# Attention and experts on one core: spreading weight scales by DMA and loading raw weights in halves

## The chip, the cores and the metric

The kernel runs on one core of a Trainium2 chip. The metric is the device time of one execution in microseconds (us). The engines are named as the profile names them: PE (matmuls), DVE (VectorE), ACT (ScalarE), POOL (GpSimd) and SP (SyncE, which here only issues DMAs).

## What is computed

A block-sparse attention over 4 batches, 8 heads, 768 tokens and 64 channels a head, and then a layer of 8 experts, of which every token passes through all, weighted by a balanced matrix P.

```python
scores = scale * np.matmul(q, k.transpose(0, 1, 3, 2))
scores = np.where(mask, scores, -1000000000.0)
attn = softmax(scores)                       # over keys
x = (attn @ v) as (3072, 512)
P = exp(logits - max); 8 times: P /= row sums, P /= column sums, P *= N / E
for e in range(8):
    h = np.maximum(x @ w1[e], 0.0)           # w1[e] is 512 x 1024
    ye = h @ w2[e]                           # w2[e] is 1024 x 512
    out += P[:, e:e + 1] * ye
```

(The reference's softmax and the balancing are shortened here; in all else it is the above in NumPy, in float32.)

## The kernel before

The attention comes first, written out as a list of steps by time slots. It gives x, which is split into seven combinations of its quadrants (a scheme with seven products in place of eight) and stored in DRAM as pairs of float16 planes (`xd`): a high part and the rest. The experts follow. For each of the 8 experts and 4 batches (32 rounds of 384 + 384 tokens) stage 1 multiplies x by w1 and stage 2 multiplies the result h by w2, each with seven products of float16 planes, and each product as three matmuls (high by high, high by low, low by high). From the third expert on, four of the seven products of stage 1 are cut once more into seven smaller ones (`inner_product`, the matmuls of L1608; the others are L1579). The matmuls of stage 2 are L1931. DVE and ACT read the products out of PSUM, form sums, and DVE or POOL make the low planes of h (L1797, L1799, L1814).

The weights arrive in float32. For each expert and each of w1 and w2 (functions `fetch_w1` and `fetch_w2`):

- `raw_load` issues one DMA of 2 MB into the one raw buffer (L421), when all readers of the weights that stood there before are done.
- `scale_jobs` finds the largest magnitude. ACT sums magnitudes in 8 parts, one after the other (L351). DVE takes each partition's maximum of the 8 (`whole`, L438). PE transposes that column (`spread`, L357), with a PSUM bank of stage 1 (`hold("s1")`) as its target, so that each partition sees all 128. DVE takes the maximum (L444) and makes a power of two and its inverse (L445 to L451, `power`).
- POOL forms the differences and sums of the quadrants in place (L1321). `split_jobs` makes each of seven planes: ACT the high half (L1333, with the scale), DVE the low half (L1338).
- `weight_job` multiplies P's column by the two inverse scales (DVE, L1453 to L1457).

None of this stands at a fixed place. A small planner (`Plan`) gets each piece of work as a job with its engine, an assumed duration, the jobs it depends on and a deadline, goes through time, and lets each engine take the ready job with the nearest deadline. PE has two streams, stage 1 and stage 2, each in its own fixed order, and takes the head that is due first. Some jobs may go to DVE or POOL, whichever is free first. A job with `rush` goes ahead of all. The outcome is one list, and every engine runs its instructions in the order of that list. So an edit of the jobs changes the order on all engines. DMAs of SP are issued in order too: one that waits holds those behind it.

Of the kernel before, what the change touches and what calls it, by code (L numbers as in the profile page):

```python
# [9 lines left out]
F32 = mybir.dt.float32  # L10
# [10 lines left out]
P = 128  # L21
# [16 lines left out]
PREP0, PREP1, PREPD = 100, 190, 50  # L38
TWO1 = ()
LOFT = 31  # L40
STEP = 2.03
# [256 lines left out]
def tile_sparse_attention_moe(  # L298
# [117 lines left out]

    def load_w(which, e):
        src, n, w = (w1, KD, FF) if which == 1 else (w2, KF, DM)
        t = raw.tile([P, KD * FF], F32, tag="r", name=f"r{which}_{e}")
        t = t.rearrange("p (c f) -> p c f", f=w)  # L420
        nc.sync.dma_start(out=t, in_=src[e].rearrange("(c p) f -> p c f", p=P))  # L421
        wr[which] = t

    def scale_steps(which, e, vector=nc.vector, scalar=nc.scalar):
# [9 lines left out]
        def part(k):  # L434
            magnitude(scalar, m[:, k : k + 1], flat[:, k * w : (k + 1) * w])
# [16 lines left out]

        return [lambda k=k: part(k) for k in range(n)], whole, spread, power

# [137 lines left out]
    with ExitStack() as actx:  # L592
# [477 lines left out]
        def start_w():  # L1070
            load_w(1, 0)
            parts, whole, spread, power = scale_steps(1, 0)
# [63 lines left out]
    def spare(n):  # L1136
# [13 lines left out]
        [dram.tile([P, CH, DM], F32, name=f"accd_{b}_{j}") for j in range(2)] for b in range(B)  # L1150
    ]
    xsd = [dram.tile([P, NP, 2, 4, TH // 2], F16, name=f"xsd_{b}") for b in range(B)]

# [134 lines left out]
    last_s3 = [()]  # L1288
    raw_free = [()]
    pwe = {}  # L1290

    def raw_load(which, e):
        return plan.dma(lambda: load_w(which, e), 2048, raw_free[0])

    def scale_jobs(which, e, loaded):
        cell = {}

        def make():
            cell["steps"] = scale_steps(which, e)

        parts = []
# [22 lines left out]
    def tts(out, x, y, n, deps, dur, op=ALU.subtract):  # L1324
        return [
            tt(lambda k=k: out()[:, k], lambda k=k: x()[:, k], lambda k=k: y()[:, k], deps, dur, op)
            for k in range(n)
        ]

    def split_jobs(which, e, dst, src, deps):  # L1330
        s = lambda: wr["s", which]
        hi = job(
# [12 lines left out]
    def fetch_w1(e):  # L1345
# [6 lines left out]

        loaded = job({"-": 0.0}, views, (loaded,) + tuple(last_s3[0]))
# [12 lines left out]
        def inner(p, src, deps):  # L1366
# [8 lines left out]
            part = lambda l: sums[p][:, l].rearrange("p (k i) f -> p k (i f)", k=KH)  # L1375
            s = lambda: wr["s", 1]
            hi = job(
# [25 lines left out]
        put(4, q10, d_s1)  # L1403
        last_s3[0] = tuple(out[5])
        raw_free[0] = tuple(x for p in out for x in out[p])
        split_done[1, e] = out

    def fetch_w2(e, loaded=None, done=None):
# [7 lines left out]

        if e == 0 or loaded is None:
            if loaded is None:
                loaded = raw_load(2, e)
            start = job({"-": 0.0}, views, (loaded,) + tuple(last_s3[0]))  # L1420
            parts, _ = scale_jobs(2, e, start)
        else:
            start = job({"-": 0.0}, views, (loaded,))
            parts = [start]
            scaled[2, e] = start
        g = lambda k: (lambda: r[k])
        m00, m10, m01, m11, t1 = (g(k) for k in ((0, 0), (1, 0), (0, 1), (1, 1), "t1"))
        base = tuple(parts)
        out = {}
# [4 lines left out]

        d_t1 = tts(t1, m01, m00, h2, base, 0.73)
# [4 lines left out]
        d6 = tts(m01, m01, m11, h2, tuple(d_t1), 0.73)  # L1440
        six = put(6, m01, d6)
# [4 lines left out]
        last_s3[0] = tuple(four)  # L1446
        raw_free[0] = tuple(x for p in out for x in out[p])
        split_done[2, e] = out
# [438 lines left out]
    def stage2(i, t0, length):  # L1887
# [6 lines left out]
        loaded = {}  # L1894
        fresh = e == 0 or 2 <= e < NE - 1
        if not fresh:
# [230 lines left out]
```

## Time and profile before

| what | us |
|---|---|
| median of 3 runs (lowest to highest) | 2171.04 (2168.24 to 2175.3) |
| the profiled execution's own time | 2168.09 |
| its span | 2166.0 |
| PE busy | 2115.0 |
| DVE busy | 1728.0 |
| ACT busy | 1442.7 |
| POOL busy | 1168.6 |

The span runs from the first to the last instruction; the time of the execution holds some 2 us around it. An engine's busy time is the union of its instructions; a matmul's record lasts longer than the time after which the next one starts. In a row of waits stand the waiting engine, line and tile, whom it waited for, the total, the number of waits and the longest. In a row of the timeline stand start, duration, engine, line and operation, and in brackets the idle time before it and who ended it. In a row of windows stand the stretch, its length, the busy time of PE, PE's weight loads, DVE, ACT and POOL (with the number of instructions), the granted clock, the share of the DMA engines and GB/s.

### The profile page before, as it was taken

The page shows a single profiled execution, that of the slowest core. Times are in us where ns is not written, and L with a number is a line of the kernel's source. Part 1 is how long each engine was busy: PE and PEld are TensorE (multiplying, and loading weights), DVE is VectorE, ACT ScalarE, POOL GpSimd, SP SyncE. Part 2 cuts the span into 40 slices and gives each one's busy share as a digit, 9 for nine tenths or more (in the row PEclk, how much of TensorE's full clock was granted, in tenths as well). Part 3 has the DMA queues.
Part 4 walks back from the last instruction along what each step waited for, and adds up shares of the span by engine and source line. Part 5 has one row for each costly group of instructions (what it writes and reads, how often), then busy time and mean ns, then how long its engine had stood idle before and what let it go on. Part 6 is the DMA issues. An engine that isn't in the chain of part 4 may idle for free.

```text
span 2166.0 us, 51169 instructions
## 1 busy us (share of the span) xinstructions
PE 2115.0 (98%) x20620; PEld 1708.6 (79%) x20620; DVE 1728.0 (80%) x3093; ACT 1442.7 (67%) x2773; POOL 1168.6 (54%) x1343
## 2 busy tenths in 40 slices
PE   6999999899999999999999999999999999999999
PEld 3777676667777778788888888888888888888887
DVE  8878888688788878876877788778877887788776
ACT  4788888786567666666676667656665666566442
POOL 5556768465245547554655475545454545466433
PEclk9999999999999999999999999999999999999999
DMA  7667966432454643454445444545454535455421
GB/s 172 142 133 168 210 131 140 146 113 95 139 185 148 221 157 122 162 145 114 113 132 159 115 120 125 163 110 147 98 164 111 143 88 178 110 153 157 140 96 66
DMA packets 223650, 299.57 MB, mean 138 GB/s; under 512 B 134812, under 2 KB 153268, under 8 KB 223412
## 3 DMA queue, kind: packets, MB, share of 16 engines
q1 hardware_dynamic: 217088, 264.81, 41.4%
q0 software_dynamic: 5760, 31.46, 8.2%
q8 instruction: 161, 2.64, 0.5%
q14 instruction: 77, 0.63, 0.1%
q10 hardware_dynamic: 564, 0.03, 0.0%
HBM read 197.16 MB, written 67.63 MB: 122 GB/s over the span
## 4 chain that ended last, share of the span: by engine, by line
PE 89%; DVE 7%; issue 1%; DMA 1%; ACT 1%; POOL 0%; DVEq 0%; ACTq 0%; POOLq 0%; SPq 0%
PE y L1931 38%; PE p L1579 22%; PE p L1608 14%; PE u L963 4%; PE t L901 2%; PE t L898 2%; PE m L865 2%; PE m L868 2%; DVE top L874 1%; DVE acc L1970 1%; DMA qt<-qs 1%; DVE w2p L1338 1%; DVE h L1799 0%; PE u L994 0%; DVE pl L916 0%
## 5 line engine op out<-in xcount | busy, mean ns | idle before, releaser
L1931 PE MATMUL y<-w2p,h 128*128 128x256 f16 x8064 | 969.8, 273 | 3.9 <-DVE w2p L1338 2.4
L1931 PEld LDWEIGHTS <-h 128*128 128x128 f16 x8064 | 786.5, 98 | 122.8 <-issue 3.9
L1797 POOL TENSOR_TENSOR h<-pair,h 128x384 f16<-128x384 f32 x388 | 389.6, 1023 | 507.6 <-ACT h L1808 449.2
L1808 ACT ACTIVATE h<-pair 128x384 f16<-128x384 f32 x640 | 312.4, 515 | 74.6 <-DVE pair L1552 25.3
L1579 PE MATMUL p<-arena 128*128 128x384 f16 x1728 | 323.1, 326 | 1.4 <-DVE pair L1552 1.4
L1552 DVE SCALAR_TENSOR_TENSOR pair<-p,pair 128x384 f32<-128x384 f32 x384 | 213.2, 555 | 127.6 <-PE p L1579 124.5
L1970 DVE SCALAR_TENSOR_TENSOR acc<-y,spare,acc 128x256 f32<-128x256 f32 x408 | 201.7, 496 | 125.3 <-PE y L1931 123.7
L1793 ACT ACTIVATE pair<-pair 128x384 f32<-128x384 f32 x384 | 195.1, 517 | 142.1 <-DVE pair L1552 115.4
L1579 PEld LDWEIGHTS <-arena 128*128 128x128 f16 x1728 | 166.9, 98 | 83.7 <-issue 1.8
L874 DVE TENSOR_REDUCE top<-m 128x1 f32<-128x768 f32 x192 | 181.9, 951 | 49.3 <-PE m L868 48.5
L906 ACT ACTIVATE pe<-t,qk 128x768 int32<-128x768 f32 x192 | 172.3, 899 | 70.6 <-PE t L901 63.2
L1608 PEld LDWEIGHTS <-loft 128*128 128x128 f16 x2304 | 198.9, 98 | 23.8 <-issue 8.6
L1579 PE MATMUL p<-attic 128*128 128x384 f16 x1152 | 214.3, 326 | 0.0
L1958 ACT ACTIVATE acc<-y,spare 128x256 f32<-128x256 f32 (+1 forms) x180 | 97.9, 544 | 134.7 <-PE y L1931 134.3
L1608 PE MATMUL p<-loft 128*128 128x192 f16 x1728 | 176.6, 246 | 6.7 <-DVE pair L1661 3.7
L1579 PEld LDWEIGHTS <-attic 128*128 128x128 f16 x1344 | 130.6, 98 | 66.6
L1839 POOL TENSOR_TENSOR pair<-pair,pair 128x384 f32<-128x384 f32 x111 | 123.3, 1123 | 90.5 <-DVE pair L1839 72.3
L1797 POOL TENSOR_TENSOR h<-u,h 128x384 f16<-128x384 f32 x122 | 120.8, 1001 | 73.1 <-ACT h L1808 67.1
L1561 ACT ACTIVATE u<-p 128x384 f32<-128x384 f32 x216 | 105.3, 488 | 68.8 <-PE p L1608 63.0
L865 PE MATMUL m<-kt,qt 128*128 128x512 f16 (+1 forms) x384 | 127.8, 333 | 10.0 <-DMA kt<-ks 7.0
L1561 ACT ACTIVATE pair<-p 128x384 f32<-128x384 f32 x168 | 82.0, 489 | 82.7 <-PE p L1579 39.1
L1321 POOL TENSOR_TENSOR r<-r 128x256 f32<-128x256 f32 (+1 forms) x150 | 127.8, 861 | 16.2 <-DVE attic L1338 10.2
(237 smaller groups left out, 3942.6 us busy)
## 6 DMA issues: line engine op xcount, KB each, us to landing
arena<-xd SPq DMA_DIRECT2D x128, 384.0 KB, 3.3
attic<-xd SPq DMA_DIRECT2D x96, 384.0 KB, 3.3
loft<-xsd SPq DMA_DIRECT2D x96, 384.0 KB, 4.6
r<-in_moe_w_dram SPq DMA_DIRECT2D x16, 2048.0 KB, 9.5
accd<-acc POOLq DMA_DIRECT2D x40, 768.0 KB, 8.2
accd<-acc SPq DMA_DIRECT2D x16, 768.0 KB, 3.9
acc<-accd SPq DMA_DIRECT2D x16, 768.0 KB, 4.7
xd<-loft SPq DMA_DIRECT2D x28, 384.0 KB, 3.0
```

What stands on the lines that cost most here:

```text
L865: nc.tensor.matmul(sc[:, lo:hi], lhsT=qt[:, 0, c], rhs=ka[:, lo:hi], start=True, stop=False)
L874: nc.vector.tensor_reduce(out=tops[n][:, c : c + 1], in_=sc[:, :S], axis=AX.X, op=ALU.max)
L906: nc.scalar.activation(pe, sc[:, :S], AF.Exp, bias=EXP_SHIFT, scale=qk[n // 2][3])
L1552: lambda: nc.vector.scalar_tensor_tensor(out=out_(), in0=bank_(), scalar=HDOWN, in1=add(), op0=ALU.mult, op1=ALU.add),
L1561: lambda: nc.scalar.activation(out_(), bank_(), AF.Relu if relu else AF.Copy, scale=HDOWN),
L1579: nc.tensor.matmul(bk.tile[:, :TH], lhsT=w1p[p][:, l, kc, fs], rhs=xp[p][:, r, kc], start=(fresh and kc == 0 and m == 0), stop=(kc == KH - ...
L1608: nc.tensor.matmul(bk.tile[:, c * HT : (c + 1) * HT], lhsT=lhs(l, c), rhs=rhs(rr), start=(fresh and c == 0 and m == 0), stop=(m == 2), ski ...
L1793: return job({"ACT": 0.52}, lambda: nc.scalar.activation(view(), view(), AF.Relu), dep)
L1797: nc.gpsimd.tensor_tensor(out=out_, in0=x, in1=y, op=ALU.subtract)
L1808: lambda: nc.scalar.activation(h.tile[:, 0], src(), AF.Relu if relu else AF.Copy),
L1931: nc.tensor.matmul(py, lhsT=hh[i, p, kc].tile[:, l, tsl], rhs=w2p[p][:, r, kc], start=(old is None and kc == 0 and m == 0), stop=(kc == h2 ...
L1970: lambda dst=dst, src=src, t=t: nc.vector.scalar_tensor_tensor(out=dst(), in0=src(), scalar=pwe[e][:, t : t + 1] if e else 1.0, in1=dst(), ...
```

## The change

1. *Scales.* For the 15 weight matrices that the planner handles (all but the first w1), PE's transpose is gone. The column of 128 maxima is written to a DRAM tile (`peak_d`, 4 bytes a partition), and a second DMA reads it back broadcast to all partitions (`peaks`, 128 x 128). Both are issued by SP. DVE's `power` then reads `peaks` in place of a PSUM bank, and has lost `rush`.
2. *Loads.* There is one fixed raw tile, loaded by two DMAs of 1 MB, the second half of the rows first. Each half has its own list of readers that must be done (`raw_free[0]`, `raw_free[1]`). The first w1 is still loaded whole, as is the first w2.
3. *Dependencies.* The 8 magnitude parts no longer wait for each other; each waits for its half, and the parts of the second half are listed first. The differences that only read the raw weights (w1's s3, w2's t1) start when the halves have landed, without waiting for the magnitudes; those that overwrite wait for them. The scale is looked up for its own expert (`wr["s", which, e]`), as the next one may be made before the last use.
4. *ADDS* names the expert number 2 that stood in `stage2`; its value is the same.

The core of the diff:

```diff
-    def load_w(which, e):
+    def load_w(which, e, half=None):
         src, n, w = (w1, KD, FF) if which == 1 else (w2, KF, DM)
-        t = raw.tile([P, KD * FF], F32, tag="r", name=f"r{which}_{e}")
-        t = t.rearrange("p (c f) -> p c f", f=w)
-        nc.sync.dma_start(out=t, in_=src[e].rearrange("(c p) f -> p c f", p=P))
+        if "raw" not in wr:
+            wr["raw"] = raw.tile([P, KD * FF], F32, name="raw_w")
+        t = wr["raw"].rearrange("p (c f) -> p c f", f=w)
+        cs = slice(0, n) if half is None else slice(half * n // 2, (half + 1) * n // 2)
+        nc.sync.dma_start(out=t[:, cs], in_=src[e].rearrange("(c p) f -> p c f", p=P)[:, cs])
...
     def raw_load(which, e):
-        return plan.dma(lambda: load_w(which, e), 2048, raw_free[0])
+        return [
+            plan.dma(lambda j=j: load_w(which, e, j), 1024, raw_free[j]) for j in (1, 0)
+        ][::-1]
...
-        parts = []
-        last = job({"-": 0.0}, make, (loaded,))
-        for k in range(8):
-            last = job({"ACT": 0.81}, lambda k=k: cell["steps"][0][k](), (last,))
-            parts.append(last)
+        made = job({"-": 0.0}, make, (loaded[1],))
+        parts = [
+            job({"ACT": 0.81}, lambda k=k: cell["steps"][0][k](), (made, loaded[k // 4]))
+            for k in (4, 5, 6, 7, 0, 1, 2, 3)
+        ]
         whole = job({"DVE": 0.16}, lambda: cell["steps"][1](), parts)
-        bk = hold("s1", ordered=False)
-        def spread():
-            spread_bank[0] = lambda nm: bk.tile
-            cell["steps"][2]()
-        pe = job({"PE": 0.3}, spread, (whole,), take=(bk,), lag=2.0)
-        power = job({"DVE": 1.2}, lambda: cell["steps"][3](), (pe,), drop=(bk,), rush=True)
+        out_ = plan.dma(
+            lambda: nc.sync.dma_start(out=peak_d[which - 1], in_=cell["steps"][4]), 1, (whole,)
+        )
+        def back():
+            nc.sync.dma_start(
+                out=peaks[which - 1],
+                in_=peak_d[which - 1].rearrange("p one -> (p one)").unsqueeze(0).to_broadcast([P, P]),
+            )
+            wr["all", which] = peaks[which - 1]
+        in_ = plan.dma(back, 64, (out_,))
+        power = job({"DVE": 1.2}, lambda: cell["steps"][3](), (in_,))
...
-        base = tuple(parts)
-        d_s3 = tts(s3, q00, q10, KH, base, 1.27)
-        d_s1 = tts(q10, q10, q11, KH, tuple(d_s3), 1.27, ALU.add)
+        base = (seen,)
+        d_s3 = tts(s3, q00, q10, KH, (seen, loaded[0]), 1.27)
+        d_s1 = tts(q10, q10, q11, KH, tuple(d_s3) + tuple(parts), 1.27, ALU.add)
...
-        raw_free[0] = tuple(x for p in out for x in out[p])
+        raw_free[0] = tuple(x for p in (0, 4, 5) for x in out[p])
+        raw_free[1] = tuple(x for p in (1, 2, 3) for x in out[p]) + tuple(d_s1)
```

`fetch_w2` is changed in the same way. Since some DVE work is now planned at other times, 40 of the jobs that may run on either engine stand on POOL instead of DVE: 19 low planes of h, 18 pieces of the prepared x and 3 sums.

The order at three places, all at the w2 of the third expert. On PE before (`y` is stage 2's bank, `p` a bank of stage 1), between the last matmuls of a stage 2 group and those of an inner product:

```order
L1931 LDWEIGHTS h_8024
L1931 MATMUL y_8018<-w2p_8006,h_8024 128x256
L357 MATMUL p_8011<-ident,ma_w_2_13391 128x128
L1608 LDWEIGHTS attic
L1608 MATMUL p_8011<-attic 128x192
L1608 LDWEIGHTS attic
L1608 MATMUL p_8011<-attic 128x192
```

and on PE now, where the first product with the new w2 begins (`w2p_8004`; the second name of a matmul is what it streams):

```order
L1943 LDWEIGHTS h_8035
L1943 MATMUL y_8017<-w2p_8005,h_8035 128x256
L1943 LDWEIGHTS h_8040
L1943 MATMUL y_8015<-w2p_8004,h_8040 128x256
L1943 LDWEIGHTS h_8040
L1943 MATMUL y_8015<-w2p_8004,h_8040 128x256
```

No transpose stands between matmuls any more, and no bank `p` is taken for it.

On DVE before, from the last two accumulations (`acc`) through the scale (`ma_w`, `sw`, `iw`) and the expert's weights (`pc`, `pcb`, `spare`) to a sum that PE waits for (`pair` from bank `p`):

```order
L1970 SCALAR_TENSOR_TENSOR acc_8058<-y_8018,spare_10890,acc_8058 128x256
L444 TENSOR_REDUCE ma_w_2_13391<-p_8011 128x1
L445 TENSOR_SCALAR ma_w_2_13391<-ma_w_2_13391 128x1
L447 TENSOR_SCALAR ma_w_2_13391<-ma_w_2_13391 128x1
L448 RECIPROCAL sw_2_13392<-ma_w_2_13391 128x1
L450 TENSOR_SCALAR sw_2_13392<-sw_2_13392 128x1
L451 TENSOR_SCALAR iw_2_13393<-ma_w_2_13391 128x1
L1453 TENSOR_SCALAR pc_13607<-iw_2_11804,iw_2_13393 128x1
L1455 TENSOR_SCALAR pcb_13609<-inv_v,pc_13607 128x4
L1457 TENSOR_TENSOR spare_13611<-pw,pcb_13609 128x24
L1661 SCALAR_TENSOR_TENSOR pair_8045<-p_8011,u_8055 128x2x192
L1814 SCALAR_TENSOR_TENSOR h_8020<-pair_8050,h_8020 128x384
```

and on DVE now:

```order
L447 TENSOR_REDUCE ma_w_2_13202<-peaks_8069 128x1
L448 TENSOR_SCALAR ma_w_2_13202<-ma_w_2_13202 128x1
L450 TENSOR_SCALAR ma_w_2_13202<-ma_w_2_13202 128x1
L451 RECIPROCAL sw_2_13203<-ma_w_2_13202 128x1
L453 TENSOR_SCALAR sw_2_13203<-sw_2_13203 128x1
L454 TENSOR_SCALAR iw_2_13204<-ma_w_2_13202 128x1
L1982 SCALAR_TENSOR_TENSOR acc_8057<-y_8015,spare_11032,acc_8057 128x256
L1465 TENSOR_SCALAR pc_13582<-iw_2_11646,iw_2_13204 128x1
L1467 TENSOR_SCALAR pcb_13584<-inv_v,pc_13582 128x4
L1469 TENSOR_TENSOR spare_13586<-pw,pcb_13584 128x24
L1859 SCALAR_TENSOR_TENSOR p_8010<-p_8010,pair_8043 128x384
L1351 SCALAR_TENSOR_TENSOR w2p_8004<-raw_w,sw_2_13203,w2p_8004 128x1024
```

The same nine instructions stand there, but one accumulation is between them, another sum follows them, and the low part of the first w2 plane comes before the last two accumulations of the old w2, which are the next two rows. Ahead of the nine, 14 DVE instructions now lie between the local maximum (L438, now L441) and the read of the peaks; before there were nine.

On SP before, around the load of that w2 (`r` is the raw buffer, `xd` and `xsd` are x planes in DRAM, `accd` the sums in DRAM):

```order
L421 DMA r_2_13171<-in_moe_w_dram 128x8x512
L472 DMA attic<-xd_77 128x1536
L1486 DMA loft<-xsd_8068 128x1536
L472 DMA arena<-xd_77 128x1536
L1998 DMA accd_1_8066<-acc_8057 128x1536
L472 DMA arena<-xd_77 128x1536
```

and on SP now:

```order
L424 DMA raw_w<-in_moe_w_dram 128x4x512
L475 DMA attic<-xd_77 128x1536
L1498 DMA loft<-xsd_8071 128x1536
L475 DMA arena<-xd_77 128x1536
L1316 DMA peak_d_8067<-ma_w_2_13202 128x1
L475 DMA arena<-xd_77 128x1536
L1320 DMA peaks_8069<-peak_d_8067 128x128
L475 DMA attic<-xd_77 128x1536
L2010 DMA accd_1_8065<-acc_8056 128x1536
```

The load is the second of two halves (the first stands five rows above), and the two small DMAs stand among the loads of x planes, here with one of those between them.

More of the change, by code (lines that the diff above doesn't have):

```diff
@@ L39 @@
 TWO1 = ()
+ADDS = 2
 LOFT = 31
@@ L451, in power @@
             vector.tensor_scalar(inv, a, 1.0 / top, None, ALU.mult)
-        return [lambda k=k: part(k) for k in range(n)], whole, spread, power
+        return [lambda k=k: part(k) for k in range(n)], whole, spread, power, a
     KB = 1024
@@ L1071, in start_w @@
             load_w(1, 0)
-            parts, whole, spread, power = scale_steps(1, 0)
+            parts, whole, spread, power, _ = scale_steps(1, 0)
             WORK.update((part, (0.0, 0.8, 0.0)) for part in parts)
@@ L1151, in tile_sparse_attention_moe @@
     ]
+    peak_d = [dram.tile([P, 1], F32, name=f"peak_d_{n}") for n in range(2)]
+    peaks = [sk.tile([P, P], F32, name=f"peaks_{n}") for n in range(2)]
     xsd = [dram.tile([P, NP, 2, 4, TH // 2], F16, name=f"xsd_{b}") for b in range(B)]
@@ L1288, in tile_sparse_attention_moe @@
     last_s3 = [()]
-    raw_free = [()]
+    raw_free = {0: (), 1: ()}
     pwe = {}
     def raw_load(which, e):
-        return plan.dma(lambda: load_w(which, e), 2048, raw_free[0])
+        return [
+            plan.dma(lambda j=j: load_w(which, e, j), 1024, raw_free[j]) for j in (1, 0)
+        ][::-1]
     def scale_jobs(which, e, loaded):
@@ L1299, in make @@
             cell["steps"] = scale_steps(which, e)
[L1301 to L1314 removed]
+            wr["s", which, e] = wr["s", which]
+        made = job({"-": 0.0}, make, (loaded[1],))
[3 more added lines that the diff above has]
+        ]
+        whole = job({"DVE": 0.16}, lambda: cell["steps"][1](), parts)
+        out_ = plan.dma(
[9 more added lines that the diff above has]
+        power = job({"DVE": 1.2}, lambda: cell["steps"][3](), (in_,))
         scaled[which, e] = power
@@ L1330, in split_jobs @@
     def split_jobs(which, e, dst, src, deps):
-        s = lambda: wr["s", which]
+        s = lambda: wr["s", which, e]
         hi = job(
@@ L1351, in views @@
             a["s3"] = wr["s3"]
-        loaded = job({"-": 0.0}, views, (loaded,) + tuple(last_s3[0]))
+        seen = job({"-": 0.0}, views, (loaded[1],) + tuple(last_s3[0]))
         parts, power = scale_jobs(1, e, loaded)
@@ L1375, in inner @@
             part = lambda l: sums[p][:, l].rearrange("p (k i) f -> p k (i f)", k=KH)
-            s = lambda: wr["s", 1]
+            s = lambda: wr["s", 1, e]
             hi = job(
@@ L1403, in fetch_w1 @@
         put(4, q10, d_s1)
-        last_s3[0] = tuple(out[5])
-        raw_free[0] = tuple(x for p in out for x in out[p])
+        last_s3[0] = tuple(out[5]) + tuple(d_s4)
+        raw_free[0] = tuple(x for p in (0, 4, 5) for x in out[p])
+        raw_free[1] = tuple(x for p in (1, 2, 3) for x in out[p]) + tuple(d_s1)
         split_done[1, e] = out
@@ L1415, in views @@
             r["t1"] = raw.tile([P, h2, DH], F32, tag="s3", name=f"t1_{e}")
[L1417 to L1421, printed above, removed]
-        else:
-            start = job({"-": 0.0}, views, (loaded,))
-            parts = [start]
-            scaled[2, e] = start
+        if loaded is None:
+            loaded = raw_load(2, e)
+        else:
+            loaded = [loaded, loaded]
+        seen = job({"-": 0.0}, views, (loaded[1],) + tuple(last_s3[0]))
+        parts, _ = scale_jobs(2, e, loaded)
         g = lambda k: (lambda: r[k])
         m00, m10, m01, m11, t1 = (g(k) for k in ((0, 0), (1, 0), (0, 1), (1, 1), "t1"))
-        base = tuple(parts)
+        base = (seen,)
         out = {}
@@ L1433, in put @@
             return out[p]
-        d_t1 = tts(t1, m01, m00, h2, base, 0.73)
+        d_t1 = tts(t1, m01, m00, h2, (seen, loaded[0]), 0.73)
         one = put(1, m10, base)
@@ L1439, in fetch_w2 @@
         five = put(5, m00, d5)
-        d6 = tts(m01, m01, m11, h2, tuple(d_t1), 0.73)
+        d6 = tts(m01, m01, m11, h2, tuple(d_t1) + tuple(parts), 0.73)
         six = put(6, m01, d6)
@@ L1446, in fetch_w2 @@
         last_s3[0] = tuple(four)
-        raw_free[0] = tuple(x for p in out for x in out[p])
+        raw_free[0] = tuple(x for p in (0, 5, 6) for x in out[p]) + tuple(d3)
+        raw_free[1] = tuple(x for p in (1, 2, 3) for x in out[p]) + tuple(d5) + tuple(d6)
         split_done[2, e] = out
@@ L1894, in stage2 @@
         loaded = {}
-        fresh = e == 0 or 2 <= e < NE - 1
+        fresh = e == 0 or ADDS <= e < NE - 1
         if not fresh:
```

## The prediction

> **What bounds the kernel now.** I read the page first, for who is busy and who ends last.
>
> ```profile
> span 2166.0 us, 51169 instructions
> PE 2115.0 (98%) x20620; PEld 1708.6 (79%) x20620; DVE 1728.0 (80%) x3093; ACT 1442.7 (67%) x2773; POOL 1168.6 (54%) x1343
> PE 89%; DVE 7%; issue 1%; DMA 1%; ACT 1%; POOL 0%; DVEq 0%; ACTq 0%; POOLq 0%; SPq 0%
> ```
>
> PE is busy for 98% of the span and is 89% of the chain that ended last. So the kernel is a stream of matmuls, and an edit gains only if it takes instructions out of PE's queue or shortens a stall of PE. The change touches the expert stage alone, so next I asked for the busy time of that stretch, and then for what PE waited for.
>
> ```profile
> 437.00:2164.00 1727.00, 1706.78 (x15139) 1418.30 (x15137) 1373.25 (x2513) 1105.85 (x2296) 900.82 (x944) 1.00 0.46 135
> PE p L1608 <- DVE u L1645: 5.7, 5, 2.7
> PE p L1608 <- DVE pair L1661: 4.2, 5, 2.6
> PE y L1931 <- DVE w2p L1338: 2.4, 2, 1.9
> PE p L1608 <- DVE ma_w L444: 0.7, 1, 0.7
> ```
>
> In 1727.0 us PE is busy 1706.8 (the first number behind the length), so all its idle time there is 20.2 us. That is the ceiling for stalls, plus a little for slowed clock. The named waits are all for DVE: none is for a weight DMA. DVE is busy for 1373 of the 1727 us, so it has room on average, and PE stalls where DVE has a knot. I therefore looked for knots that the scaling of weights makes.
>
> **Term 1, the transposes.** Fifteen PE transposes of the weights' peaks leave PE's queue.
>
> ```profile
> L357 PE MATMUL p<-ident,ma_w 128*128 128x128 f32 x15 | 4.1, 273 | 0.0
> 441.44 0.27 PE L357 MATMUL p<-ident,ma_w 128*128 128x128 f32 x1
> 441.55 0.98 PE L1579 MATMUL p<-arena,attic 128*128 128x384 f16 x5
> ```
>
> A record lasts 273 ns, but the next matmul starts 0.11 us later, so a transpose costs PE 0.11 us. Fourteen make 1.5 us; the fifteenth is in term 2. The bounds are 1.5 and the 4.1 of the group's busy time. I take 1.5, because the starts show what the queue pays.
>
> **Term 2, the knot at 898 us**, where the scale of the third expert's w2 is made. PE first, then DVE, then the clock.
>
> ```profile
> 898.62 0.27 PE L357 MATMUL p<-ident,ma_w 128*128 128x128 f32 x1
> 899.55 0.66 PE L1608 MATMUL p<-attic 128*128 128x192 f16 x6 [0.67 <-DVE ma_w L444]
> 902.84 0.96 PE L1608 MATMUL p<-loft 128*128 128x192 f16 x6 [2.63 <-DVE pair L1661]
> 904.50 0.37 PE L1931 MATMUL y<-w2p,h 128*128 128x256 f16 x1 [0.48 <-DVE w2p L1338]
> 900.36 0.21 DVE L1453 TENSOR_SCALAR pc<-iw,iw 128x1 f32<-128x1 f32 x1
> 900.61 0.83 DVE L1455 TENSOR_SCALAR pcb<-inv_v,pc 128x4 f32<-128x4 f32 x1
> 901.47 0.84 DVE L1457 TENSOR_TENSOR spare<-pw,pcb 128x24 f32<-128x24 f32 x1
> 902.24 0.55 DVE L1661 SCALAR_TENSOR_TENSOR pair<-p,u 128x384 f32<-128x384 f32 x1
> 900.00:910.00 10.00, 6.89 (x60) 5.77 (x58) 9.03 (x18) 5.91 (x9) 5.63 (x8) 0.83 0.20 80
> ```
>
> The transpose holds a PSUM bank until DVE's L444 has read it, so the next product waits 0.67 us. Then DVE works through the scale and the three instructions of the expert's weights (to 902.3) before L1661, for which PE waits 2.63 us; then 0.48 more for the w2 plane. That is 3.78 us of idle. Behind it the granted clock of these 10 us is 0.83, which loses 1.7 us more. So the knot costs about 5.5 us. In the new order no PSUM bank is held, and the same nine DVE instructions stand further ahead of the plane's first product, with one accumulation among them. They are not gone: nine instructions and a 1.3 us plane still stand in a row ahead of that product. I leave 1.2 us of stall there and take a gain of 4.3; the bounds are 0 (the knot only moves) and 5.5.
>
> The Trainium skill, "TensorE: Matmul & The Clock Gate", section on the HAM clock gate, says that the clock halves after at least one idle window of about 3.4 us. By that rule gaps of 2.6 us would cost no clock and this term would be an estimated 2.6 instead of 4.3; the trace differs, since 0.83 follows a gap of 2.63 us, and I go by the trace.
>
> **Term 3, two smaller stalls tied to weights.**
>
> ```profile
> 719.93 0.70 PE L1931 MATMUL y<-w2p,h 128*128 128x256 f16 x5 [1.90 <-DVE w2p L1338]
> 717.94 1.94 DVE L1338 SCALAR_TENSOR_TENSOR w2p<-t,sw,w2p 128x1024 f16<-128x1024 f32 x1
> 1118.54 0.66 PE L1608 MATMUL p<-attic 128*128 128x192 f16 x6 [0.28 <-DVE pair L1661]
> 1120.06 0.66 PE L1608 MATMUL p<-loft 128*128 128x192 f16 x6 [0.86 <-DVE pair L1661]
> ```
>
> The first is a w2 plane of the second expert whose low part DVE began only as PE asked for it. Halves that are freed and loaded separately let the magnitudes start earlier, so I expect the planes earlier: bounds 0 and 1.9, taken 1.0. The second (1.14 us) comes behind the same block of DVE instructions, one expert on: bounds 0 and 1.1, taken 0.6.
>
> **What I cost at nothing, and its cover.** The magnitudes on ACT and the differences on POOL stay in number; they may start after a half has landed instead of after the whole or after all magnitudes. About 40 instructions go from DVE to POOL (low halves of h, and of the prepared x). A low half costs POOL more than DVE:
>
> ```profile
> L1797 POOL TENSOR_TENSOR h<-pair,h 128x384 f16<-128x384 f32 x388 | 389.6, 1023 | 507.6 <-ACT h L1808 449.2
> L1799 DVE SCALAR_TENSOR_TENSOR h<-pair,h 128x384 f16<-128x384 f32 x124 | 93.3, 764 | 3.8 <-ACT h L1808 3.8
> ```
>
> POOL takes 1.02 us against 0.76. PE's work on other planes hides it, and POOL idles half the time. Were the cover gone, 40 times 0.26 us is 10 us. The DVE time that is freed (40 times at most 0.76, 30 us) is worth nothing by itself, as DVE has 20% to spare.
>
> **The added wait.** A peak now goes to DRAM (512 bytes in 128 pieces) and comes back as 64 KB, with SP waiting for the first landing before it issues the second. No row shows such a transfer, so the nearest ones bound it:
>
> ```profile
> arena<-xd SPq DMA_DIRECT2D x128, 384.0 KB, 3.3
> wg<-in_moe_w_gate_dram ACTq DMA_DIRECT2D x1, 16.0 KB, 3.6
> r<-in_moe_w_dram SPq DMA_DIRECT2D x16, 2048.0 KB, 9.5
> accd<-acc POOLq DMA_DIRECT2D x40, 768.0 KB, 8.2
> 1700.00:1800.00 100.00, 97.06 (x892) 83.31 (x890) 83.67 (x144) 64.02 (x132) 45.82 (x53) 0.98 0.52 146
> ```
>
> One way takes 3.3 to 3.6 us by the smallest transfers and 8.2 by POOL's queue; a round trip is 6.6 to 16.4, and I take 7.0 by the smallest. On DVE 144 instructions pass in 100 us, or 0.69 us each. The new order puts 10 to 17 DVE instructions between the local maximum and the read of the peaks for all w2 but one, and over 20 for w1: 7 to 12 us and over 14. So the trip is hidden, though barely for the shortest. If it is late, DVE waits with all that stands behind, and PE's products wait for DVE. The next x planes queue behind SP's wait; of PE's waits in the expert stage none names one of their DMAs now, so I let that cover a hold of 3.3 us (without it, up to 3.3 us each time). A half of raw weights (1 MB) should land between 3.3 and 9.5 us after its issue; nobody on PE waits for it.
>
> **Sum.** 1.5 + 4.3 + 1.0 + 0.6 = 7.4 us. The profiled execution took 2168.1 us (span 2166.0 and 2.1 around it), near the lowest of the three timed runs, 2.9 under their median 2171.0. 2168.1 - 7.4 = 2160.7, so I say 2161. All other stalls (20.2 - 3.8 - 1.9 - 1.1 = 13.4 us of idle) I keep in amount, although the new order will put them elsewhere.
>
> **Rivals.** (A) *The new order gives it back.* Every engine's order changes, and the 13.4 us come from single late DVE instructions. If the knot moves rather than opens (term 2 at 0) and the planes come no earlier, 1.5 remains: 2166.6. For it: the nine instructions are still in one piece. Against: they no longer hold a PSUM bank.
>
> (B) *POOL blocks DVE more often.* The largest stall of the later stage is of another kind:
>
> ```profile
> 1771.64 4.23 DVE L1799 SCALAR_TENSOR_TENSOR h<-u,h 128x384 f16<-128x384 f32 x1
> 1776.52 0.83 PE L1608 MATMUL p<-loft,attic 128*128 128x192 f16 x6 [2.69 <-DVE u L1645]
> 1770.00:1780.00 10.00, 7.30 (x56) 5.93 (x54) 9.39 (x9) 2.87 (x5) 5.45 (x7) 0.84 0.47 80
> L1338 DVE SCALAR_TENSOR_TENSOR w2p<-r,sw,w2p x48: 1267/1276/4572, 448.1 to 2019.2; 128x1024 f16<-128x1024 f32 x48
> ```
>
> An instruction of 0.76 us on average took 4.23 while POOL worked, PE idled 2.69 us and lost 1.6 us of clock behind it (0.84 of 10 us): 4.3 together. A plane's low part has 1.28 as its median and 4.57 as its longest. POOL gets 40 instructions on 1343, 3% more; one more such meeting makes 2161 + 4.3 = 2165. None fewer is as possible, since DVE has 40 fewer to be caught. The Trainium skill, "SBUF — State Buffer", "Who interferes with whom", says that DVE and GpSimd share a port pair as an exclusive lock, where an instruction of two SBUF inputs waits for the whole of the other; the 4.23 us agrees.
>
> (C) *More opens than I count.* With weights ready earlier, half of the other 13.4 us goes too: 2161 - 6.7 = 2154.
>
> (D) *Slower: DVE waits for the peaks.* Place: L444's read for the eight w2. If the trip takes R, DVE waits R - 7.6 where 11 instructions (11 x 0.69) cover it, and I estimate that PE feels all but 1.3 us of that (two DVE instructions). The gain is gone at R = 9.8, where eight stalls cost 7.4 us. At 12 us they cost 8 x 3.1 = 24.8: 2185. For it: 128 separate pieces, behind 384 KB transfers. Against: no row of SP's small loads is over 5 us.
>
> **Chances.** Forecast 0.50, A 0.22, B 0.10, C 0.12, D 0.06. A measurement of this kernel can tell about 0.3%, 6.5 us, from no change; against the median 2171.0 that is under 2164.5. Of the forecast 0.45 lies there, and all of C: faster 0.57. B, most of A and the rest make 0.34 for no difference. D and 0.03 of A, with added stalls, are slower: 0.09. The range takes in C's lower end (2151) and A at the median's level (2172); D and the far ends of A and C are left out.
>
> **What would show it.** Right: no product waits around a w2's scale, the clock stays at 1.00 in the tenth of the span near 900 us, and PE's idle time from 437 us on falls to about 13 us. Term 2 is wrong if a wait over 2 us stands behind L1457's counterpart; the added wait is mis-sized if DVE idles before the read of the peaks. A gain of more than 15 us would mean that the weights' lateness cost more than PE's waits name.

## The result, and the profile after

| | before | after |
|---|---|---|
| median of 12 runs each, on one chip (us) | 2167.52 (2166.32 to 2175.3) | 2179.55 (2175.38 to 2190.75) |
| the profiled execution (us) | 2168.09 | 2180.49 |
| its span (us) | 2166.0 | 2178.6 |

After / before is 1.0056, with a 95% interval of 1.0041 to 1.0071: the change made the kernel slower by 0.56%. The prediction was 2161, faster, with a range up to 2172.

The page of the changed kernel, first the span and the busy times, then the chain that ended last, by engine and by line:

```profile
span 2178.6 us, 51353 instructions
PE 2117.1 (97%) x20605; PEld 1708.3 (78%) x20605; DVE 1714.8 (79%) x3053; ACT 1443.4 (66%) x2773; POOL 1202.2 (55%) x1383
PE 87%; DVE 6%; DMA 4%; issue 1%; ACT 1%; POOL 0%; SPq 0%; DVEq 0%; ACTq 0%; POOLq 0%
PE y L1943 38%; PE p L1591 21%; PE p L1620 14%; PE u L966 4%; PE t L904 2%; PE t L901 2%; PE m L868 2%; PE m L871 2%; DMA peak_d<-ma_w 2%; DMA peaks<-peak_d 1%; DVE top L877 1%; DMA qt<-qs 1%; PE u L997 0%; DVE pair L1851 0%; DVE pl L919 0%
```

PE's busy time is nearly the same (2117.1 against 2115.0, with 15 instructions fewer), and DVE has 13 us less to do. POOL has 34 us more, the instructions that went over to it. So the two engines that the chain mostly runs over have no more work: the span grew by waiting. The chain says whose: DMA was 1% of it and is 4%, and the two small transfers of the peaks make 3%.

The expert stage as one window (with the same columns as before), the waits that name those transfers, and the groups of DMAs (KB each, median us to landing), all of the changed kernel:

```profile
437.00:2177.00 1740.00, 1709.49 (x15120) 1418.12 (x15118) 1360.10 (x2472) 1105.70 (x2295) 930.96 (x978) 1.00 0.48 134
DVE ma_w L447 <- DMA peaks<-peak_d: 36.4, 10, 6.7
PE p L1620 <- DVE pair L1695: 7.7, 5, 2.9
PE p L1620 <- DVE u L1657: 7.6, 8, 1.4
PE p L1591 <- DVE pair L1564: 4.1, 2, 3.5
raw_w<-in_moe_w_dram SPq DMA_DIRECT2D x28, 1024.0 KB, 5.2
peaks<-peak_d SPq DMA_DIRECT2D x15, 64.0 KB, 5.4
peak_d<-ma_w SPq DMA_DIRECT2D x15, 0.5 KB, 7.3
```

PE idles 1740.0 - 1709.5 = 30.5 us in the stage; it was 20.2. A small write takes 7.3 us to land and the read-back 5.4, so the trip is 12.7 at the medians. In 10 of the 15 scales DVE idles before L447, the read of the peaks, 36.4 us in all. (L447 is L444 of before.)

The place of the prediction's term 2, the third expert's w2, from the timelines of SP, DVE and PE of the changed kernel, and then its window:

```profile
890.35 0.15 DVE L441 TENSOR_REDUCE ma_w<-mx_w 128x1 f32<-128x8 f32 x1
890.53 0.32 SPq L1316 DMA_DIRECT2D peak_d<-ma_w  x1
898.81 0.32 SPq L1320 DMA_DIRECT2D peaks<-peak_d  x1
903.60 0.29 DVE L447 TENSOR_REDUCE ma_w<-peaks 128x1 f32<-128x128 f32 x1 [4.65 <-DMA peaks<-peak_d]
905.88 0.27 PE L1943 MATMUL y<-w2p,h 128*128 128x256 f16 x1 [2.09 <-ACT w2p L1346]
906.09 1.28 DVE L1351 SCALAR_TENSOR_TENSOR w2p<-raw_w,sw,w2p 128x1024 f16<-128x1024 f32 x1
907.43 1.86 PE L1943 MATMUL y<-w2p,h 128*128 128x256 f16 x8 [1.28 <-DVE w2p L1351]
906.00:911.00 5.00, 3.72 (x22) 2.63 (x21) 5.00 (x11) 4.91 (x9) 1.38 (x2) 0.66 0.64 258
```

The local maximum is ready at 890.4, 3.5 us sooner than in the timeline of before (893.85), and then 13 us go by until the scale can be made. DVE stands idle for 4.65 us of that. PE waits for the plane that needs the scale, first its high half (ACT) and then its low half (DVE), 3.37 us together, and the clock behind it is 0.66 for 5 us. PE's row names ACT and a plane; only DVE's row one step back names the DMA.

The last w2 shows the other way in which it reaches PE: the sum `pair` stands behind L447 in DVE's order and has nothing to do with the scale.

```profile
1982.98 0.28 DVE L447 TENSOR_REDUCE ma_w<-peaks 128x1 f32<-128x128 f32 x1 [4.34 <-DMA peaks<-peak_d]
1984.00 0.55 DVE L1695 SCALAR_TENSOR_TENSOR pair<-p,u 128x384 f32<-128x384 f32 x1
1984.60 0.66 PE L1620 MATMUL p<-arena,loft 128*128 128x192 f16 x6 [2.94 <-DVE pair L1695]
450.13 2.08 PE L1591 MATMUL p<-attic 128*128 128x384 f16 x6 [3.47 <-DVE pair L1564]
1551.28 0.66 PE L1620 MATMUL p<-arena,loft 128*128 128x192 f16 x6 [2.35 <-DVE pair L1695]
1769.22 0.66 PE L1620 MATMUL p<-arena,loft 128*128 128x192 f16 x6 [1.56 <-DVE pair L1695]
1335.58 0.66 PE L1620 MATMUL p<-arena 128*128 128x192 f16 x6 [1.14 <-ACT pair L1573]
449.00:457.00 8.00, 6.87 (x25) 3.37 (x25) 7.85 (x13) 5.06 (x10) 1.86 (x2) 0.57 0.47 167
1551.00:1556.00 5.00, 4.72 (x34) 3.95 (x34) 3.30 (x7) 4.68 (x7) 1.40 (x2) 0.66 0.69 186
1767.00:1777.00 10.00, 8.44 (x85) 7.62 (x83) 9.20 (x23) 7.41 (x13) 4.29 (x6) 1.00 0.84 222
1985.00:1989.00 4.00, 4.00 (x28) 3.22 (x26) 3.25 (x7) 4.00 (x8) 1.31 (x2) 0.57 0.68 150
```

The rows below them are the other places where PE stands still behind such a read, and the clock: it falls behind the stalls that end at 450, 1551 and 1985 us, and stays at 1.00 behind the short one that ends at 1769. The idle time there sums to 3.47 + 3.37 + 1.14 + 2.35 + 1.56 + 2.94 = 14.8 us. The clock loses 8 x 0.43 + 5 x 0.34 + 5 x 0.34 + 4 x 0.43 = 8.6 us. Together that is 23.4 us, where before lost 5.5 us at 900 and 4.3 at 1774: 13.6 us more, against the 12.0 that were measured. Smaller stalls differ too, so the sum isn't exact.

### The profile page after: what moved, and what is told of

The parts are those of the page before. It is cut to its first block, busy times and chain, and to the rows that moved or that the text cites. A ratio compares the mean times of both kernels' runs of the same rounds, so it can differ in the third digit from the quotient of the medians.

```text
span 2178.6 us, 51353 instructions
## 1 busy us (share of the span) xinstructions
PE 2117.1 (97%) x20605; PEld 1708.3 (78%) x20605; DVE 1714.8 (79%) x3053; ACT 1443.4 (66%) x2773; POOL 1202.2 (55%) x1383
## 4 chain that ended last, share of the span: by engine, by line
PE 87%; DVE 6%; DMA 4%; issue 1%; ACT 1%; POOL 0%; SPq 0%; DVEq 0%; ACTq 0%; POOLq 0%
PE y L1943 38%; PE p L1591 21%; PE p L1620 14%; PE u L966 4%; PE t L904 2%; PE t L901 2%; PE m L868 2%; PE m L871 2%; DMA peak_d<-ma_w 2%; DMA peaks<-peak_d 1%; DVE top L877 1%; DMA qt<-qs 1%; PE u L997 0%; DVE pair L1851 0%; DVE pl L919 0%
## 5 line engine op out<-in xcount | busy, mean ns | idle before, releaser
L1809 POOL TENSOR_TENSOR h<-pair,h 128x384 f16<-128x384 f32 x413 | 414.8, 1025 | 442.0 <-ACT h L1820 371.6
L1620 PEld LDWEIGHTS <-loft 128*128 128x128 f16 x2304 | 198.4, 98 | 25.2 <-issue 11.1
L1620 PE MATMUL p<-loft 128*128 128x192 f16 x1728 | 176.6, 246 | 1.9 <-DVE u L1657 1.1
L1334 POOL TENSOR_TENSOR raw_w<-raw_w 128x256 f32<-128x256 f32 (+1 forms) x150 | 127.8, 862 | 56.1 <-DVE attic L1351 24.2
L1809 POOL TENSOR_TENSOR h<-u,h 128x384 f16<-128x384 f32 x116 | 112.8, 978 | 67.4 <-ACT h L1820 60.1
```

The source lines that it names most:

```text
L1620: nc.tensor.matmul(bk.tile[:, c * HT : (c + 1) * HT], lhsT=lhs(l, c), rhs=rhs(rr), start=(fresh and c == 0 and m == 0), stop=(m == 2), ski ...
L1809: nc.gpsimd.tensor_tensor(out=out_, in0=x, in1=y, op=ALU.subtract)
```

## The experiments

The theory (**T**): the trip through DRAM is longer than the work that DVE has between the local maximum and the read of the peaks. DVE stands still, and PE waits for what is queued behind the read. The first rival (**O**): the trip is incidental, and the new order with 40 instructions moved to POOL sets the time. Ratios are to the kernel before, on the same chip, with 95% intervals. The first four kernels shared one set of runs of before (median 2168.77), the next four another (2167.81), the last two a third (2168.72).

**1. All of the change but the trip.** The changed kernel with PE's transpose, its PSUM bank and the rush put back.

```diff
-        out_ = plan.dma(lambda: nc.sync.dma_start(out=peak_d[which - 1], in_=cell["steps"][4]), 1, (whole,))
...
-        in_ = plan.dma(back, 64, (out_,))
-        power = job({"DVE": 1.2}, lambda: cell["steps"][3](), (in_,))
+        bk = hold("s1", ordered=False)
+        def spread():
+            spread_bank[0] = lambda nm: bk.tile
+            cell["steps"][2]()
+        pe = job({"PE": 0.3}, spread, (whole,), take=(bk,), lag=2.0)
+        power = job({"DVE": 1.2}, lambda: cell["steps"][3](), (pe,), drop=(bk,), rush=True)
```

> The changed kernel with the scale spread by PE's transpose again (whole, transpose, L444 with its rush), all else as changed: halves, freer dependencies, the order that follows. Theory T (the trip of the peaks through DRAM is longer than the order covers, DVE waits for it and PE behind DVE): the 36 us of DVE's waits for the peaks are gone and with them the PE stalls and the half clock behind them, some 17 + 8 us; 2155 to 2164 us, at or below the kernel before (2167.5). Rival O (the new order of the freed work, with 40 more POOL instructions, makes the stalls): 2174 to 2180, near the changed kernel's 2179.6.

Measured: 2162.48 us, ratio 0.9968 (0.9956 to 0.9979). Without the trip the rest of the change is faster than before. Its window of the stage and of the 15 us around 900, the same 15 us of before, and the scale of that w2 in the experiment's timeline:

```profile
437.00:2160.00 1723.00, 1706.31 (x15148) 1418.06 (x15145) 1364.34 (x2481) 1106.10 (x2300) 918.62 (x974) 1.00 0.46 135
895.00:910.00 15.00, 14.82 (x141) 12.62 (x140) 14.90 (x26) 11.43 (x25) 10.24 (x12) 1.00 0.54 167
```

```profile
895.00:910.00 15.00, 11.22 (x103) 9.67 (x101) 13.49 (x29) 10.58 (x21) 10.63 (x14) 0.89 0.32 116
```

```profile
886.63 0.15 DVE L441 TENSOR_REDUCE ma_w<-mx_w 128x1 f32<-128x8 f32 x1
890.20 0.28 DVE L447 TENSOR_REDUCE ma_w<-p 128x1 f32<-128x128 f32 x1
```

The knot at 900 is gone: 14.82 of 15 us busy at clock 1.00, against 11.22 at 0.89. By PE's transpose the peaks were read 3.6 us after the local maximum, where the trip needed 13.

**2. The trip alone.** The kernel before with only the transposes replaced by the two DMAs (the edit of experiment 1 turned round, in before.)

> The kernel before with only the spread of the scales by two small DMAs, without the halves and the freer dependencies. T: DVE waits 2 to 7 us for the peaks at most of the 15 matrices, PE stalls behind, 2175 to 2190 us. O: within 4 us of the kernel before, 2164 to 2171.

Measured: 2211.01 us, ratio 1.0199 (1.0183 to 1.0214), worse than either theory had it. Its waits:

```profile
DVE ma_w L444 <- DMA peaks<-peak_d: 43.3, 9, 7.4
PE p L1615 <- DVE pair L1690: 16.0, 10, 6.3
PE p L1615 <- DVE pair L1668: 10.2, 4, 6.6
```

Here the magnitudes come late: the local maximum of the third expert's w2 stands at 898.95 us, against 890.35 in the changed kernel. DVE's waits are only a little longer in sum (43.3 against 36.4), but more of each reaches PE: 26 us in the two groups, with single waits of over 6 us. Behind the two longest stalls the granted clock is 0.53 for 11 us (from 911 on) and 0.51 for 14 us (from 1133 on).

**3. Room for the trip.** The changed kernel, where the planner is told to leave time for the two transfers. It assumes 2.0 us for a landing (`DMA_LAND`) and so plans some 5 us for the trip; this adds 12.5.

```diff
-        power = job({"DVE": 1.2}, lambda: cell["steps"][3](), (in_,))
+        in_.lag = 6.5
+        power = job({"DVE": 1.2}, lambda: cell["steps"][3](), (in_,), lag=6.0)
```

> The changed kernel, with 6.5 us more assumed by the planner between the write's landing and the read-back and 6 us more before the read of the peaks, so that DVE's read stands later in its order and nothing else is edited. T: DVE's idle time before the read falls from 36 us to under 8, the time to 2156 to 2168. O: the DMAs are there and so is the kind of order, 2174 to 2182. A third way out: the later scale makes the weight planes late and PE waits for w2 planes instead, 2172 or more with waits on L1346 or L1351.

Measured: 2167.16 us, ratio 0.9993 (0.9983 to 1.0002). No wait of DVE for the peaks is left among the waits, with the same two DMAs in place. PE waits for planes instead, since the scale is now later than it has to be:

```profile
PE y L1944 <- DVE w2p L1352: 5.6, 7, 1.3
```

**4. A first look at why the write is slow.** The changed kernel with further small DMAs that nothing reads, of five kinds in turn.

> The changed kernel with one more small DMA to DRAM behind each scale, which nobody waits for, of five kinds in turn (three of each): 128 x 4 bytes side by side on SP, 128 x 4 bytes 512 bytes apart, 128 rows of 512 bytes, one row of 512 bytes, 128 x 4 bytes side by side on ACT's queue. The write of the peaks took 7.3 us to land although its packets had all begun 2 us after the issue. If 4-byte pieces that share 512 bytes of DRAM are what is slow: 7 us for the first and the fifth kind and 2 to 4 us for the others. If any piece under 512 bytes is: 7 us for the second as well. If it is the load on SP's ring: 4 us or more for the third and fourth, less for the fifth.

Measured: 2177.56 us in one run; DVE waited 35.6 us for the peaks. The groups mix the kinds (one name for several, with a median of 5.0 us for the 512-byte ones), but the kinds come in turn, so a single landing can be told by its place. One of the first kind (issued at 1549.5 us), two of the second (557.2 and 1119.8) and one of the third (1766.2):

```profile
probe<-ma_w SPq DMA_DIRECT2D x1, 0.5 KB, 7.3
probe<-ma_w SPq DMA_DIRECT2D x1, 0.5 KB, 1.4
probe<-ma_w SPq DMA_DIRECT2D x1, 0.5 KB, 5.0
probe<-peaks SPq DMA_DIRECT2D x1, 64.0 KB, 1.5
```

The view has a landing for only one more, of the third kind (2.0). For the others the trace keeps the 16 signals that report a DMA; the last of them comes after 8.4 and 8.6 us for the first kind, 8.8, 9.0 and 14.9 for the fifth (ACT's queue), 4.1 for the second and 4.1 for the third. The fourth kind, one row, wasn't read. So all six writes of 4-byte pieces side by side took 7.3 us or more, and all six of the second and third kind 5.0 or less. It isn't that the pieces are small, since the second kind has the same 128 pieces of 4 bytes: it is that they lie side by side. That is what the expectation had for pieces that share 512 bytes of DRAM. It rests on one run with three of each kind, and which distance is enough wasn't tried.

**5. The write on another queue.** The changed kernel with the 512-byte write issued by ACT.

```diff
-            lambda: nc.sync.dma_start(out=peak_d[which - 1], in_=cell["steps"][4]), 1, (whole,)
+            lambda: nc.scalar.dma_start(out=peak_d[which - 1], in_=cell["steps"][4]), 1, (whole,),
+            eng="ACT",
```

> The changed kernel, with only the 512-byte write of the 128 maxima issued by ACT's queue in place of SP's; the read-back stays on SP. Theory L (the layout: 128 pieces of 4 bytes set the landing): the write still lands about 7 us after its issue, DVE still idles over 20 us before the read of the peaks, time 2174 to 2184. Rival Q (SP's queue: the write lands late because it shares a queue with the loads of x planes and of raw weights): it lands within 4 us, the trip falls to about 9 us, DVE idles under 10 us there, time 2164 to 2170. ACT may lose up to 1 us for each issue, 15 us in all on an engine that is busy for two thirds, which neither theory lets PE see.

Measured: 2182.09 us, ratio 1.0065 (1.0051 to 1.0079). Its groups of DMAs and its wait:

```profile
peaks<-peak_d SPq DMA_DIRECT2D x15, 64.0 KB, 5.0
peak_d<-ma_w ACTq DMA_DIRECT2D x15, 0.5 KB, 8.0
DVE ma_w L447 <- DMA peaks<-peak_d: 36.5, 12, 4.3
```

The write is no faster on a queue with almost nothing else in it (8.0 against 7.3), so SP's queue isn't the reason. What is left are the layout and the DMA engines that all queues share. The first write of the peaks in the changed kernel bears on the engines: it is issued at 432.89 us, its packets all begin between 433.7 and 433.9, and it lands at 440.2. All packets of the core between 434 and 440 us:

```profile
DMA packets 0, 0.00 MB, mean 0 GB/s; under 512 B 0, under 2 KB 0, under 8 KB 0
```

So this write took its 7.3 us with no other transfer beside it. The changed kernel's other writes to DRAM bear on the layout:

```profile
accd<-acc POOLq DMA_DIRECT2D x40, 768.0 KB, 8.5
accd<-acc SPq DMA_DIRECT2D x16, 768.0 KB, 4.2
xd<-loft SPq DMA_DIRECT2D x28, 384.0 KB, 2.9
out_dram<-acc SPq DMA_DIRECT2D x16, 384.0 KB, 2.7
```

SP's writes of 384 and 768 KB land in 2.7 to 4.2 us, sooner than these 512 bytes in 128 pieces. With the kinds of experiment 4, that leaves the layout.

**6. One load in place of the halves.** The kernel of experiment 1 with the raw weights in one DMA of 2 MB.

```diff
-        return [
-            plan.dma(lambda j=j: load_w(which, e, j), 1024, raw_free[j]) for j in (1, 0)
-        ][::-1]
+        one = plan.dma(lambda: load_w(which, e), 2048, tuple(raw_free[0]) + tuple(raw_free[1]))
+        return [one, one]
```

> The first experiment's kernel (all of the change but the DMA spread, PE transposes back) with the raw weights loaded again by one DMA of 2 MB, released when all readers are done. What is left of the change is the freed dependencies and the order. If the halves carry the gain (2162.5 against 2169.3, 6.8 us), the time returns to 2167 to 2171. If the dependencies and the order carry it, it stays at 2161 to 2165. The load's landing should be near 9.5 us and the halves' 5.2 us are gone. PE's wait for the second expert's plane near 720 us (2.6 us in the first experiment) should not be shorter than there.

Measured: 2166.94 us, ratio 0.9995 (0.9986 to 1.0004): no gain is left. The knot at 900 is back, as its timeline of DVE and PE and its window show:

```profile
895.42 0.15 DVE L441 TENSOR_REDUCE ma_w<-mx_w 128x1 f32<-128x8 f32 x1
905.28 0.96 PE L1614 MATMUL p<-loft 128*128 128x192 f16 x5 [2.44 <-DVE pair L1667]
895.00:910.00 15.00, 11.06 (x92) 9.90 (x91) 12.90 (x30) 10.93 (x21) 10.28 (x10) 0.81 0.39 132
```

The local maximum stands at 895.4, against 886.6 with halves. The wait near 720 us was 1.8 us here and 2.4 with halves, so that one owes nothing to them.

**7. Less room.** Experiment 3 with both lags at 3 us, so that the planner allows about 11 us for the trip.

> The third experiment's kernel with both added lags cut to 3 us (from 6.5 and 6), so that the planner allows about 11 us for the trip (2 times 2 us of landing, 0.5 us of the transfers' own time, 6 us of lag) in place of 5 and of 17.5. The trip measured 12.6 us at the median. Theory T: DVE waits a little before some reads (under 10 us in all, against 36 without lags and none named with the long ones), PE's wait for late w2 planes falls from 5.6 to about 3 us, time 2162 to 2167. Rival O (the order and POOL's load set the time, not the trip): no trend with the lag, time 2167 to 2180.

Measured: 2163.95 us, ratio 0.9984 (0.9975 to 0.9994). Both sides of the trade stand among its waits, the read that is a little too early and the planes that are a little late:

```profile
DVE ma_w L447 <- DMA peaks<-peak_d: 4.3, 5, 1.3
PE y L1944 <- DVE w2p L1352: 2.8, 3, 1.3
```

**8. Named probes.** The changed kernel with four small DMAs behind each scale, which nothing reads, each kind with a name of its own (`flat_d`, `apart_d`, `rows_d`, `act_d`).

> The changed kernel with four more small DMAs behind each of the 15 scales, which nothing reads, each with a target name of its own: flat_d (128 times 4 bytes, one behind the other, SP), apart_d (128 times 4 bytes, 512 bytes apart, SP), rows_d (128 rows of 512 bytes, SP) and act_d (as flat_d, by ACT's queue). Theory L (many 4-byte pieces set the landing): flat_d, apart_d and act_d all land at about 5 to 8 us, rows_d at 1.5 to 3. If it is that the pieces lie in the same 512 bytes of DRAM: flat_d and act_d 5 to 8, apart_d 1.5 to 3. If it is SP's queue: act_d under 4, the three others over 5. The time is not the point of it: 2174 to 2190.

Measured: 2174.36 us in one run. All four kinds showed 8.9 to 10.5 us, the 64 KB in rows too, which had taken 1.5 to 4.1 in experiment 4. But here `apart_d` was issued 0.4 to 6.2 us behind its `flat_d`, each time before that one had landed, and the other two behind it. So the landings hang together, and this run can't tell the kinds apart. What it did show is by accident: its order left more room, DVE waited 24.9 us for the peaks in place of 36.4, and the time of this one run is below all 12 of the changed kernel (2175.38 at the lowest).

**9. Halves with the old dependencies.** The kernel of experiment 1, but the magnitudes one after the other, and the differences behind all of them.

```diff
...
-            job({"ACT": 0.81}, lambda k=k: cell["steps"][0][k](), (made, loaded[k // 4]))
+            last = job({"ACT": 0.81}, lambda k=k: cell["steps"][0][k](), (last, loaded[k // 4]))
...
-        base = (seen,)
+        base = (seen,) + tuple(parts)
...
```

> The first experiment's kernel (halves, PE transposes) with the old dependencies: the 8 magnitude parts one after the other, and the differences that read the raw weights after all magnitudes. With one load and the new dependencies the time was that of before (2166.9, ratio 0.9995), with both it was 2162.5 (0.9968). Theory H (the halves alone bring the magnitudes forward): 2161 to 2164.5, ratio 0.996 to 0.998, and the local maximum of the third expert's w2 stands near 887 us, as in the first experiment (886.6), against 893.9 before. Rival J (halves and freed dependencies only work together): 2165 to 2168, local maximum after 891 us, and a stall of over 2 us at 898 to 906 us.

Measured: 2178.58 us, ratio 1.0043 (1.003 to 1.0057). Neither theory had that. The local maximum of the third expert's w2 stands at 882.5 and the knot at 900 is gone, as theory H said. But PE idles 27.3 us of the window that has 16.7 in experiment 1, at other places. The window, and the largest of these stalls from the timelines of DVE and PE:

```profile
437.00:2160.00 1723.00, 1695.71 (x15038) 1407.26 (x15037) 1372.16 (x2475) 1105.46 (x2299) 927.21 (x977) 1.00 0.46 134
1774.44 6.31 DVE L1346 SCALAR_TENSOR_TENSOR w2p<-raw_w,sw,w2p 128x1024 f16<-128x1024 f32 x1
1781.27 0.66 PE L1615 MATMUL p<-loft 128*128 128x192 f16 x6 [3.55 <-DVE u L1652]
```

An instruction that takes 1.28 us as a rule took 6.31, while POOL worked until 1779.7. Another 3.5 us go at 719 to 722.5 us, behind a run of DVE's operations on `loft`. So without any trip an order can cost as much as the trip does. Why this one does, rather than that of experiment 1, stays open.

**10. Without the rush.** The kernel of experiment 1 without `rush=True`.

> The first experiment's kernel with the rush of the scale's chain on DVE taken away, as the change took it. In the changed kernel the trip and the lost rush came together; this tells them apart. Theory T (the trip alone is the loss): 2161 to 2165. Rival (the lost rush is part of the loss): the PSUM bank that the transpose holds comes free later, PE waits more for banks at the scales, 2166 to 2175.

Measured: 2164.75 us, ratio 0.9978 (0.9969 to 0.9988). With PE's transpose the rush is worth 0.0010 of the time (about 2 us), and the two intervals overlap, so the lost rush is at most a small part of the change's loss. With the DMAs it wasn't tried.

Side by side, with DVE's idle time before the read of the peaks (all that a kernel's waits name):

| kernel | peaks by | halves | new dependencies | DVE waits (us) | ratio |
|---|---|---|---|---|---|
| changed | DMA | yes | yes | 36.4 | 1.0056 |
| 5 (ACT queue) | DMA | yes | yes | 36.5 | 1.0065 |
| 7 (lags of 3) | DMA | yes | yes | 4.3 | 0.9984 |
| 3 (lags of 6.5 and 6) | DMA | yes | yes | none | 0.9993 |
| 1 | PE | yes | yes | - | 0.9968 |
| 10 (no rush) | PE | yes | yes | - | 0.9978 |
| 6 | PE | no | yes | - | 0.9995 |
| 9 | PE | yes | no | - | 1.0043 |
| 2 | DMA | no | no | 43.3 | 1.0199 |

Experiment 1 has the lowest ratio, and is faster than both kernels; its interval overlaps those of experiments 10 and 7. The two single runs (4 and 8) are left out.

## Why the prediction was wrong

**The step that failed is the sizing in "The added wait"**: "a round trip is 6.6 to 16.4, and I take 7.0 by the smallest". The trip is 12.7 at the medians. The bounds held it; the choice between them didn't. It went by the sizes of the transfers: the smallest rows (384 KB in 3.3, 16 KB in 3.6) stood for the smallest transfer. By experiment 4 it is not the size that sets the time of the write but how its pieces lie (7.3 us or more side by side, 1.4 to 5.0 with 512 bytes between their starts). With 12.7 in place of 7.0 the next sentence, "the trip is hidden, though barely", turns round: 10 to 17 DVE instructions cover 7 to 12 us. For the w1, counted with 14 us of cover, it failed too at four places, where the read-back took up to 9.4 us. The prediction named the sign of it, "the added wait is mis-sized if DVE idles before the read of the peaks", and DVE idles there 10 times.

**Rival D had the mechanism, and nearly the price.** It put eight stalls at 24.8 us for a trip of 12 us; the profile shows six at 23.4 us with the clock. Not all eight, since the reads at 678 and 1118 us found their peaks there. That the two sums are so near is luck: D counted two stalls too many and no clock, which is 8.6 of the 23.4. Its chance of 0.06 came from "no row of SP's small loads is over 5 us". Those rows are loads of long rows of memory, and the write in question is 128 pieces of 4 bytes side by side. D had named the pieces as what speaks for it.

**That the trip is the cause** rests on three things together: the waits name it in the changed kernel; with the DMAs kept and time allowed for them the time comes back (1.0056 to 0.9984 and 0.9993, experiments 7 and 3); and by PE's transpose it comes back as far or further (0.9968). Rival O would have left those at the changed kernel's level. But experiment 9 warns of reading one pair of kernels alone, since other dependencies, and the order that follows from them, cost 16 us there.

**Term 1** (1.5 us) can't be seen: the kernel with the 15 transposes is the fastest.

**Term 2** (gain 4.3) is nought in the changed kernel: where 3.78 us of idle and 1.7 of clock were lost there are 3.37 and 1.7, behind another wait. By itself the term was right and rather small: in experiment 1 the 15 us around 900 gain 14.82 - 11.22 = 3.6 us of work, and the clock 15 x 0.11 = 1.7. Its reason was wrong, though. "No PSUM bank is held" isn't it, for experiment 1 holds the bank and has no knot. Halves bring the local maximum from 893.9 or 895.4 (before, experiment 6) to 882.5 to 890.4 (9, 1 and the changed kernel), and in 9 and 1 the scale is then done before the first product asks for it.

**Term 3**: the wait at 719.9 fell from 1.9 to 0.6 us in the changed kernel, but 1.5 us for another sum stand at 714, and in experiment 1 the wait is 2.4 us. The two at 1118 to 1120 are gone in both. A gain of at most about 1 us of the 1.6 is all that can be said.

**What was costed at nothing.** POOL's added work may not have been free: the waits of `p L1620` for `u`, 7.6 us in 8 pieces, stand in five of the 8 places behind a single DVE instruction that took 2 to 3 us longer than usual while POOL was busy, as rival B had it, with many small meetings in place of one large. But the same group was 5.7 us in 5 pieces before, so at most some 2 us are new, and how much of that is due to the 40 instructions wasn't measured apart. The freed dependencies by themselves gain nothing (experiment 6). Whether the halves need them isn't shown: without them (9) the local maximum comes early and the knot is gone all the same, and what is lost is lost at other places.

**The clock.** The prediction weighed a rule of the Trainium skill, "TensorE: Matmul & The Clock Gate", section on the HAM clock gate, against the row of a 2.63 us gap, and went by the row. The changed kernel bears that out: the clock fell behind gaps of 2.35 and 2.94 us as well, and stayed at 1.00 behind 1.56. But the length of a gap alone doesn't decide it: in experiment 9 it stayed at 1.00 behind the gap of 3.54 us that ends at 722.5, and in experiment 2 it was 0.66 for 5 us behind one of 1.94 us at 1798.

## What to carry to other kernels

Before a hand-over is moved from an engine to a DMA, price the whole trip from the maker's last instruction to the reader's first, not the transfer. Here PE's transpose took 3.6 us and 0.11 us of PE's queue, the trip by DRAM 12.7 us. Where a planner places the reader, tell it the measured trip: with about 11 us in place of 5, the same DMAs took 0.9984 of the time before in place of 1.0056. And ask how the pieces lie in DRAM: 512 bytes apart, the write alone took 1.4 to 5.0 us in place of 7.3; the kernel with such a write wasn't tried. When the waiting engine's row names another engine, look one row further back: here the cause stood only in DVE's wait.

## What was not expected of the hardware

- 512 bytes in 128 pieces of 4 bytes side by side take longer to land than 768 KB in long rows by the same queue (7.3 against 4.2 us), and no less by ACT's queue (8.0). With the pieces 512 bytes apart it was 1.4 to 5.0 us (experiment 4). The Trainium skill, "DMA: Bandwidth & Descriptors", section on the anatomy of one DMA, has about 2.0 us as the fixed cost of a DMA of POOL's path, most of it the receipt from the memory written. On SP's path the first write of the peaks spent 6.3 of its 7.3 us behind the start of its last packet, far above that. In its section on queues, rings and completion order the same page says that the signal of completion lands only after every earlier write of the same DMA engine, across its queues. That would fit a write that is late on both queues, but for the first write of the peaks it isn't the reason: the core's last write before it had landed 7.7 us before it was issued. In experiment 8, `apart_d` landed after the `flat_d` ahead of it each time, which agrees with the rule.
- A low half of a w2 plane, 1.28 us as a rule, took 6.31 us in experiment 9. It ended at 1780.75, 1.1 us after the end of six POOL instructions that followed one another from 1774.25 to 1779.66. The 4.23 us that rival B shows ended 0.4 us after such a run too (at 1775.45 in the kernel before). No POOL instruction in the two runs took over 1.2 us, so these are delays by a whole run of them and not by one.
- The planner's assumed landing of 2.0 us is below the measured median of every group of loads and writes of the changed kernel above. No wait of PE in its expert stage names the x planes or the raw weights (3.3 and 5.2 us), so there it doesn't matter; the peaks had no such slack.
